# Moving the scan's short matrix products within the steps of a fused scan and feed-forward kernel

## The chip, the core and the metric

The kernel runs on one core of a Trainium2 chip. The metric is the device time of one execution in microseconds (us). A profiled execution also has a span, the time from its first to its last instruction. Engines are named as in the profile: PE multiplies matrices (PEld is its loading of the stationary operand), DVE, ACT and POOL work element by element, SP issues DMA transfers.

## The reference

A state-space scan feeds a feed-forward layer with a cosine gate. There are 4 sequences, 8 heads, 768 positions, 32 channels a head and a state of 16:

```python
for c in range(nc):
    L = np.exp(cum[:, :, :, None] - cum[:, :, None, :]) * causal
    M = np.einsum('bhin,bhjn->bhij', Cc, Bc) * L
    y[:, :, sl] = (np.einsum('bhij,bhjd->bhid', M, xc)
                   + np.einsum('bhin,bhnd->bhid', Cc, state) * np.exp(cum)[:, :, :, None])
    state = decay_full * state + np.sum(Bx, axis=2)
...
h = x @ w_in                 # 3072 x 256 times 256 x 2048
g = h * np.cos(h)
out = g @ w_out              # 3072 x 2048 times 2048 x 256
```

The x of the second part is the y of the first, with heads side by side. All is in float32.

## The kernel before, in words

The 768 positions are cut into 6 chunks of 128, each of two units of 64 positions. For each chunk c the feed-forward layer takes 16 steps f, numbered n = 16 c + f. While the steps of chunk c run, the scan of chunk e = c + 1 is worked out between their instructions. The order on every engine is written out by hand: an engine takes its instructions in the order in which the program issues them.

**One step (period7, from n = 33 on).** The products of a step are done in a form with 7 multiplications in place of 8 (Strassen's), for the first matrix (hp) and for the second (o). Step n begins hp of step n (begin7, L775: three products), then issues the first two products of o of step n - 3 (first_, L846), the last two of hp of step n - 1 (rest7[n - 1][2]), then o's next (then), the middle two of hp of step n (rest7[n][0]), and o's rest (last_). On the other engines the step finishes n - 1: ACT rounds hp to whole turns (wind_k, L682), DVE subtracts (wind_w, L688), ACT takes the sine (gate, L697), DVE multiplies (gated, L702: gT), POOL forms differences (L727, L729, L730: gd). For its own hp, ACT copies partial sums (L779, L780) and DVE adds them (L783, L785). On DVE the order in a step is wind_w(n - 1), L783 and L785 of n, gated(n - 1).

**Banks.** hp of steps 11, 12, 13 and 14 lie in two banks by turns, so begin7 of step 13 waits until gT of step 11 is done, and step 14 until that of step 12. Step 5 waits for gT of step 3. hp of steps 9, 10 and 15 lie in two pairs of banks that y and g use too: y's first pair is that of step 9, its second that of step 10.

**The scan's visits.** Products of the scan are short (64 columns and fewer) and come in groups of 32, which the profile shows as 64 passes. Step 5 holds inner2 (L614: g = B C of both units). Step 13 holds open2 (L628: y from the state and rT, the decayed C; then sums, L478: the new states, not for the last chunk), which stands ahead of begin7. take_ahead (L490) has ACT copy those states. finish2 (L640: y from the masked weights m) has two halves, one before last_ and one behind it, each followed by take_y (L649, ACT copies y to yT), the first also by differ_y (L757, POOL). A visit in the text is what steps 5 and 12 to 14 of one chunk hold: visit A is that of c = 2, B of c = 3, C of c = 4; C has no sums.

**Work beside it.** scan_work lists by step what else the scan does: turn_blocks (L585, DVE transposes), mask_c (L592, ACT), reaches (L575, DVE scan), reach_c (L597, DVE: rT), add_state (L501 and L503, DVE: state), weights (L466, DVE: m), half_decay (L376, DVE: half a scan of decays; its last quarter also issues load_arow, a POOL memset at L162 and two transfers on SP at L164, and weigh0 on POOL, L382). load_blocks (L146, L149) brings B and C in pieces, one a step. The sums of a finished o are added on POOL (L891), one a step, and stored by SP (L894).

Of the kernel before, what the change touches and what calls it, by code (L numbers as in the profile page):

```python
# [25 lines left out]
def kernel(  # L26
# [13 lines left out]
    V, ACT, G, PE = nc.vector, nc.scalar, nc.gpsimd, nc.tensor  # L40
# [3 lines left out]
    P = 128  # L44
    NC = S // P
    DM, DF = moe_w_in.shape
    KT = DM // P
    NF = DF // P
# [573 lines left out]
    def open2(c):  # L622

        ys[c] = y = [pair("y") for _ in range(2)]
        for k, p, s, q in ((k, p, s, q) for k in range(2) for p in range(2) for s in range(2)
                           for q in range(4)):
            r, o_, i = group(q, s), W * (q % 2), (2 * k + p) * W
            PE.matmul(y[s][o_:o_ + W, q // 2, i:i + W], lhsT=after[2 * c + k - 1][r, s, p],  # L628
                      rhs=rTs[c, s][r, p, k * W:(k + 1) * W], start=(k == p == 0), stop=False,
                      tile_position=(r.start, o_), skip_group_check=True)  # L630
        for k in range(2 if c < NC - 1 else 0):
            sums(2 * c + 1 + k, [y[s][:, 0, (2 + k) * P:(3 + k) * P] for s in range(2)], group)

    def finish2(c, ks=(0, 1)):

# [453 lines left out]
        gate(n)  # L1089
        gated(n)  # L1090

    def period7(n, extra=(), begin=(), early=(), end=((), ())):

        for do in begin:
            do()
        begin7(n, bank_of(n))
        while finished:
            finished.pop()()
        first_, then, last_ = seven(n - LAG)
        first_()  # L1100
        if n - 1 in sevens:
            rest7[n - 1][2]()
            wind_k(n - 1)
        then()
        rest7[n][0]()
        for do in early:
            do()
        if n - 1 in sevens:
            wind_w(n - 1)
        rest7[n][1]()  # L1110
        if n - 1 in sevens or n - 1 in late:
            gate(n - 1)
            gated(n - 1)
        for do in end[0]:
            do()
        last_()
        for do in end[1]:
            do()
        for do in extra:
            do()  # L1120

# [52 lines left out]
    for n in range(AHEAD, 2 * NF):  # L1174
        c, f = divmod(n, NF)
        if n < NC * NF:

            if c == 1 and 6 <= f <= 9:
                load(c + 2, f - 6)
            if n in (NF - 4, NF - 3):  # L1180
                load_arow(n - NF + 8)
            if n == NF - 2:
                for k in (4, 5):
                    for s in range(2):
                        load_x(k, s)
            if n in (NF - 1, NF):
                load_along(2, (2 * (n == NF), 2 * (n == NF) + 1))
            for e, i in chunks_at(n, "along"):
                load_along(e + 1, (2 * i, 2 * i + 1))
            first(n)  # L1190
            closing = n == 2 * NF - 1
            if closing:
                finish2(c + 1)
            wind_k(n)
            wind_w(n)
            if closing:
                take_y(c + 1, 0)
            for e, s in chunks_at(n - 1, "turn"):
                turn2(e, s)
            for k in units_at(n, 2):  # L1200
                turn_unit(k)
            if n + 1 in piece:
                rests_of.append(grade(*piece[n + 1], later=True))
            gate(n)
            while len(rests_of) > (n == AHEAD):
                rest = rests_of.pop(0)
                if rest:
                    rest()
            joins = n in piece and piece[n] in held
# [12 lines left out]
            if not joins and behind:  # L1222
                behind.pop(0)()
            gated(n)
            if closing:
                take_y(c + 1, 1)
                take_ahead(c + 1)
                for i in range(4):
                    differ_y(2, i, G, slice(0, 1))
            if n == NF + 7:  # L1230
                weigh0(5)
            if add_s and (n == NF - 5 or units_at(n - 1, 4)):
                exchange = add_s()
                add_s = None
            if n == NF + 9:
                exchange()
            for do in behind:
                do()
            if f not in ((10, 11, 12) if c == 1 else (10, 11)):
                for do in unsummed:  # L1240
                    do()
                unsummed.clear()
            for k, ((_, last_), *_) in unit_at.items():
                if last_ == n:
                    weigh0(k)
        for i, js in differ_at.get(n, ()):
            differ_w(i, js)
        for at in in_at.get(n, ()):
            differ_in(*at)
        if n == AHEAD + 1:  # L1250
            second(n - LAG)
        if n > AHEAD and n != LATER:
            second(n - (LAG if n > LATER else LAG - 1))
        for e, _ in chunks_at(n, "inner"):
            inner2(e)
        for k in units_at(n, 3):
            for t in range(2):
                inner(k, t)
            if k == 3:
                at = [gs[k, s][:, 0, 2 * P:] for s in range(2)]  # L1260
                sums(4, at, group)
                take_sums((4,), at)
            weights(k, 0)
        for k in units_at(n, 4):
            take_s, add_s = finish0(k)
            take_s()
        for k in units_at(n, 1):
            reach_unit(k)
        if n == 2 * NF - 3:
            open2(c + 1)  # L1270
        load_more(n)

    def visit_g(n, e):

        period7(n, begin=[lambda: inner2(e)],
                early=[lambda: weights(2 * e, 0), lambda: weights(2 * e + 1, 0),
                       lambda: weights(2 * e, 1)])

    def visit_y(n, e):

        halves = [lambda i=i: half_decay(2 * e + 3, i // 2, i % 2)
                  for i in range(4 if e < NC - 1 else 0)]

        def taken(k):
            finish2(e, (k,))
            take_y(e, k)
            if k == 0:
                for i in range(4):
                    differ_y(e, i, G, slice(0, 1))

        period7(n, halves[3:], begin=[lambda: open2(e), lambda: take_ahead(e)],
                early=halves[:3], end=[[lambda k=k: taken(k)] for k in range(2)])

    def half_decay(k, p, i):

# [7 lines left out]
    def scan_work(c, f):  # L1303
# [9 lines left out]
                7: [lambda: add_state(2 * e, (1,))],  # L1313
                11: [lambda: turn_blocks(e + 1, 0, (1,))],
                12: [lambda: turn_blocks(e + 1, 0, (0,))]}
        if c == 2:
            work[0] = [lambda: add_state(5), lambda: turn_blocks(e, 0)]
            work[1] = [lambda: turn_blocks(e, 1, (1,)), lambda: mask_c(e, 0, 0),
                       lambda: mask_c(e, 0, 1)]
            work[2] = [lambda: turn_blocks(e, 1, (0,)), lambda: mask_c(e, 1, 0),  # L1320
                       lambda: mask_c(e, 1, 1)]
            work[3] = [lambda: reaches(e, 0)]
            work[4] = [lambda: reaches(e, 1)]
            work[6] = [lambda: weights(2 * e + 1, 1), lambda: reach_c(e, 0)]
            work[7] = [lambda: add_state(2 * e, (0,))]
            work[11] = [lambda: add_state(2 * e, (1,)), *work[11]]
            work[12] = [lambda: reach_c(e, 1), *work[12]]
        for i in range(4 if e < NC - 1 else 0):
            work.setdefault(7 + i, []).append(lambda i=i: half_decay(k, i // 2, i % 2))
        if e == NC - 1:  # L1330
# [4 lines left out]
    for n in range(2 * NF, NC * NF + LAG):  # L1335
# [8 lines left out]
        extra = scan_work(c, f) if live else ()  # L1344
        if n >= NC * NF:
            second(n - LAG)
        elif live and f == 5:
            visit_g(n, e)
        elif live and f == 13:
            visit_y(n, e)  # L1350
        elif n in sevens:
            period7(n, extra)
        else:
            first(n, rest7[n - 1][2] if n - 1 in sevens else None, to_=bank_of(n))
            if n - 1 in sevens:
# [48 lines left out]
```

## Time and profile before

| | |
|---|---|
| median of 3 runs | 368.54 us (368.35 to 368.97) |
| the profiled execution | 368.55 us |
| its span | 366.5 us, so 2.05 us lie around it |
| mean granted clock of PE | 0.995 |
| PE busy | 354.1 us |
| PEld, DVE, ACT, POOL busy | 330.1, 273.2, 213.9, 252.5 us |

The profile of the execution gives its instructions with start and duration, and in brackets the idle time of the engine just before one and what ended it. "issue" there means that the engine waited for nothing that the profile shows. One product of 128 columns appears as two passes, each a weight load and a matmul. A windows line gives, for a stretch of the span, its length, the busy time of PE, PEld, DVE, ACT and POOL with the number of instructions, PE's granted clock, the share of the DMA engines and GB/s. Times in the text are microseconds from the start of the span; times "from the start of step 12" count from 171.71 in visit A, 233.26 in B and 290.52 in C.

### The profile page before, as it was taken

What the parts mean: (1) busy time and instruction counts of PE and PEld (TensorE: products, weight loads), DVE (VectorE), ACT (ScalarE), POOL (GpSimd) and SP (SyncE); (2) the same over time, 40 slices, a digit from 0 to 9 for tenths busy, and PEclk for the clock granted to TensorE, in tenths of its full rate; (3) what the DMA queues carried; (4) which work ended last, traced back from release to release, by engine and by line L of the source; (5) the groups of instructions that cost most, each with busy time, mean ns of one, the idle gap of its engine ahead of it and who ended that gap; (6) DMA issues with size and microseconds to landing.
All of it is one profiled execution on the core that took longest, in us unless ns stands there. A gap on an engine that the chain in (4) does not pass through costs nothing.

```text
span 366.5 us, 10731 instructions
## 1 busy us (share of the span) xinstructions
PE 354.1 (97%) x4268; PEld 330.1 (90%) x4268; DVE 273.2 (75%) x479; ACT 213.9 (58%) x446; POOL 252.5 (69%) x410
## 2 busy tenths in 40 slices
PE   8999999999999999999599999989999999999995
PEld 5788888898989899999599999989999989999995
DVE  7799998578687947898558889868887646666663
ACT  4588766454455267467356756656746746666751
POOL 6567667879869987957555765765776565685671
PEclk9999999999999999999989999999999999999999
DMA  7996957673765147023307103101001001001011
GB/s 142 289 341 147 209 134 90 121 115 76 137 91 92 41 99 96 10 65 75 75 13 104 25 0 71 27 4 38 0 2 31 2 2 31 3 0 30 2 29 29
DMA packets 97328, 26.46 MB, mean 72 GB/s; under 512 B 87328, under 2 KB 93184, under 8 KB 97280
## 3 DMA queue, kind: packets, MB, share of 16 engines
q1 hardware_dynamic: 96032, 25.41, 34.7%
q8 instruction: 33, 0.54, 0.7%
q10 hardware_dynamic: 1248, 0.39, 0.5%
q14 instruction: 15, 0.12, 0.1%
HBM read 22.38 MB, written 3.34 MB: 70 GB/s over the span
## 4 chain that ended last, share of the span: by engine, by line
PE 77%; DVE 6%; POOL 5%; SPq 4%; ACT 4%; issue 3%; DMA 1%; DVEq 0%; POOLq 0%; ACTq 0%
PE o L846 26%; PE hp L775 19%; PE hp L675 17%; PE o L805 7%; DVE gT L702 2%; PE y L640 2%; POOL gd L727 2%; SPq L188 2%; ACT w L697 2%; DVE w L688 2%; SPq L149 1%; ACT k L682 1%; PE y L478 1%; POOL gd L729 1%; POOL gd L730 1%
## 5 line engine op out<-in xcount | busy, mean ns | idle before, releaser
L688 DVE SCALAR_TENSOR_TENSOR w<-hp,k 128x512 f32<-128x512 f32 x96 | 66.0, 688 | 63.4 <-ACT k L682 62.8
L727 POOL TENSOR_TENSOR gd<-gT 128x256 f32<-128x256 f32 x79 | 63.7, 806 | 70.6 <-DVE gT L702 60.2
L697 ACT ACTIVATE w<-w,quarter 128x512 f32<-128x512 f32 x96 | 69.3, 722 | 67.6 <-DVE w L688 67.5
L682 ACT ACTIVATE k<-hp 128x512 int32<-128x512 f32 x96 | 57.4, 598 | 39.2 <-PE hp L675 25.1
L702 DVE TENSOR_TENSOR gT<-hp,w 128x512 f32<-128x512 f32 x96 | 66.0, 687 | 17.7 <-ACT w L697 13.5
L846 PE MATMUL o<-words,gd 128*128 128x128 f32 x474 | 76.6, 277 | 0.0
L675 PE MATMUL hp<-yT,w_in 128*128 128x256 f32 x280 | 66.8, 383 | 0.3 <-DVE gT L702 0.3
L846 PEld LDWEIGHTS o<-words,gd 128*128 128x128 f32 x474 | 64.3, 192 | 0.3 <-issue 0.2
L775 PE MATMUL hp<-m,wid 128*128 128x128 f32 x366 | 61.1, 276 | 0.2 <-ACT hp L780 0.2
L675 PEld LDWEIGHTS hp<-yT,w_in 128*128 128x128 f32 x280 | 51.4, 190 | 7.9 <-POOL mag L250 0.7
L846 PE MATMUL o<-w_out,gT 128*128 128x128 f32 x316 | 49.7, 276 | 2.0 <-issue 2.0
L775 PEld LDWEIGHTS hp<-m,wid 128*128 128x128 f32 x366 | 50.6, 192 | 0.4 <-ACT hp L780 0.3
L775 PE MATMUL hp<-yT,w_in 128*128 128x128 f32 x244 | 48.1, 279 | 2.9 <-DVE gT L702 1.7
L846 PEld LDWEIGHTS o<-w_out,gT 128*128 128x128 f32 x316 | 43.3, 192 | 3.0 <-issue 2.2
L729 POOL TENSOR_TENSOR gd<-gT,gd 128x128 f32<-128x128 f32 x79 | 39.2, 496 | 6.2
L730 POOL TENSOR_TENSOR gd<-gT,gd 128x128 f32<-128x128 f32 x79 | 38.0, 481 | 6.2
L775 PEld LDWEIGHTS hp<-yT,w_in 128*128 128x128 f32 x244 | 37.2, 192 | 4.0 <-issue 1.8
L779 ACT COPY m<-hp 128x256 f32<-128x256 f32 x61 | 22.5, 368 | 15.9 <-PE hp L775 15.5
L846 PE MATMUL o<-w_out,gd 128*128 128x128 f32 x158 | 30.8, 277 | 0.0
L846 PE MATMUL o<-words,gT 128*128 128x128 f32 x158 | 30.8, 277 | 0.0
L805 PE MATMUL o<-w_out,gT 128*128 128x256 f32 x128 | 29.9, 379 | 0.0
L376 DVE TENSOR_TENSOR_SCAN lam<-arow,unit 128x256 f32<-128x256 f32 (+1 forms) x28 | 29.3, 1058 | 0.0
(126 smaller groups left out, 557.2 us busy)
## 6 DMA issues: line engine op xcount, KB each, us to landing
words<-in_moe_w_in_dram SPq DMA_DIRECT2D x8, 512.0 KB
words<-in_moe_w_out_dram SPq DMA_DIRECT2D x8, 512.0 KB
xr<-in_x_dram SPq DMA_DIRECT2D x24, 128.0 KB
arow<-a_cut SPq DMA_DIRECT2D x10, 256.0 KB
arow<-a_cut SPq DMA_DIRECT2D x10, 252.0 KB
out_dram<-sum SPq DMA_DIRECT2D x18, 128.0 KB
bc<-in_B_dram SPq DMA_DIRECT2D x24, 64.0 KB
along<-a_all SPq DMA_DIRECT2D x8, 65.0 KB
```

Source lines behind the costliest of these rows:

```text
L376: V.tensor_tensor_scan(out=lams[k][:, p, hs].rearrange(flat), data0=rows_.rearrange(flat), data1=unit0[:, hs].rearrange(flat), initial=0.0 ...
L675: PE.matmul(to_[:, e], lhsT=w_in[:, k, fs], rhs=y[:, k], start=(k == 0), stop=(k == KT - 1), skip_group_check=True)
L682: ACT.activation(k, hp[n], AF.Copy, bias=0.25, scale=INV_2PI)
L688: V.scalar_tensor_tensor(out=w, in0=hp[n], scalar=INV_2PI, in1=k, op0=ALU.mult, op1=ALU.subtract)
L697: ACT.activation(cos, cos, AF.Sin, bias=quarter, scale=TWO_PI)
L702: V.tensor_tensor(out=gT[n], in0=hp.pop(n), in1=cos, op=ALU.mult)
L727: G.tensor_tensor(out=d[:, 0:2], in0=g[:, 1:2].to_broadcast([P, 2, P]), in1=g[:, 3::-3], op=ALU.subtract)
L729: G.tensor_tensor(out=d[:, 2], in0=g[:, 0], in1=d[:, 0], op=ALU.subtract)
L730: G.tensor_tensor(out=d[:, 3], in0=g[:, 2], in1=d[:, 2], op=ALU.subtract)
L775: PE.matmul(at[:, i], lhsT=w[q], rhs=y_[q], start=(q == 1), stop=True, skip_group_check=True)
L805: PE.matmul(o[c, u][:, t], lhsT=g[:, 2 * e + t], rhs=w_out[:, 2 * j + e], start=(j == e == t == 0), stop=(j == NJ - 1 and e == 1), skip_gr ...
L846: PE.matmul(at[q], lhsT=a_[q], rhs=w[q], start=(j == 0 and q in starts), stop=(j == NJ - 1), skip_group_check=True)
```

## The change

- period7 loses its end hooks and gets mid (behind rest7[n - 1][2] and wind_k) and o_first: with it the first two products of o stand ahead of begin7 instead of behind it.
- Step 5: o_first; inner2 stays where it was.
- Step 12: open2 without the sums (L628) runs at mid.
- Step 13: o_first. The sums (L478, now sums2) and take_ahead come ahead of it; the first half of finish2 (L640), its take_y and differ_y run at mid; two of the four half_decay stay early, the third follows the step.
- Step 14: the second half of finish2 and its take_y come first, then the first products of o (o_first); the fourth half_decay follows the step.
- c = 2 alone: reach_c(e, 1) moves from step 12 to step 8, the second half of add_state(2 e) from step 11 to step 9.
- The number of products, copies, scans and transfers is the same. open2 of chunk 2 (n = 29) is followed by its sums as before.

```diff
-        for k in range(2 if c < NC - 1 else 0):
-            sums(2 * c + 1 + k, [y[s][:, 0, (2 + k) * P:(3 + k) * P] for s in range(2)], group)
+    def sums2(c):
+        for k in range(2 if c < NC - 1 else 0):
+            sums(2 * c + 1 + k, [ys[c][s][:, 0, (2 + k) * P:(3 + k) * P] for s in range(2)], group)
...
-    def period7(n, extra=(), begin=(), early=(), end=((), ())):
+    def period7(n, extra=(), begin=(), mid=(), early=(), o_first=False):
+        first_, then, last_ = seven(n - LAG)
         for do in begin:
             do()
+        if o_first:
+            first_()
         begin7(n, bank_of(n))
         while finished:
             finished.pop()()
-        first_, then, last_ = seven(n - LAG)
-        first_()
+        if not o_first:
+            first_()
         if n - 1 in sevens:
             rest7[n - 1][2]()
             wind_k(n - 1)
+        for do in mid:
+            do()
         then()
         rest7[n][0]()
...
-        for do in end[0]:
-            do()
         last_()
-        for do in end[1]:
-            do()
...
+    def visits(n, e):
+        f = n % NF
+        if f == 5:
+            return dict(o_first=True, begin=[lambda: inner2(e)],
+                        early=[lambda: weights(2 * e, 0), lambda: weights(2 * e + 1, 0),
+                               lambda: weights(2 * e, 1)])
+        if f == 12:
+            return dict(mid=[lambda: open2(e)])
+        if f == 13:
+            return dict(o_first=True, begin=[lambda: sums2(e), lambda: take_ahead(e)],
+                        mid=[lambda: finish2(e, (0,)), lambda: take_y(e, 0)] + [
+                            lambda i=i: differ_y(e, i, G, slice(0, 1)) for i in range(4)],
+                        early=[lambda i=i: half_decay(2 * e + 3, 0, i)
+                               for i in range(2 if e < NC - 1 else 0)])
+        return {}
...
+        for i in range(2 if e < NC - 1 else 0):
+            work.setdefault(13 + i, []).append(lambda i=i: half_decay(2 * e + 3, 1, i))
...
-            work[11] = [lambda: add_state(2 * e, (1,)), *work[11]]
-            work[12] = [lambda: reach_c(e, 1), *work[12]]
+            work[8] = [lambda: reach_c(e, 1)]
+            work[9] = [lambda: add_state(2 * e, (1,))]
...
         elif n in sevens:
-            period7(n, extra)
+            at = visits(n, e) if live else {}
+            if f == 14 and c >= 2 and c < NC - 1:
+                at = dict(o_first=True, begin=[lambda: finish2(e, (1,)), lambda: take_y(e, 1)])
+            period7(n, extra, **at)
```

More of the change, by code (lines that the diff above doesn't have):

```diff
@@ L1270 @@
             open2(c + 1)
+            sums2(c + 1)
         load_more(n)
[L1273 to L1292, printed above, removed]
+    def visits(n, e):
[13 more added lines that the diff above has]
+        return {}
     def half_decay(k, p, i):
@@ L1346 @@
             second(n - LAG)
[L1347 to L1350, printed above, removed]
         elif n in sevens:
-            period7(n, extra)
+            at = visits(n, e) if live else {}
+            if f == 14 and c >= 2 and c < NC - 1:
+                at = dict(o_first=True, begin=[lambda: finish2(e, (1,)), lambda: take_y(e, 1)])
+            period7(n, extra, **at)
         else:
```

## The prediction

> **What bounds the kernel now.** I read the page first, then the waits, then each visit in the timeline of PE.
>
> ```profile
> span 366.5 us, 10731 instructions
> ...
> PE 354.1 (97%) x4268; PEld 330.1 (90%) x4268; DVE 273.2 (75%) x479; ACT 213.9 (58%) x446; POOL 252.5 (69%) x410
> ...
> q8 instruction: 33, 0.54, 0.7%
> ```
>
> PE is full, so the question is where its few idle microseconds lie. Busy time by stretches (length, PE, PEld, DVE, ACT, POOL, clock, DMA) shows it: steps 12 to 14 of visits A, B, C, then step 5 of A, a step without a visit, and a stretch of A.
>
> ```profile
> 171.70:190.50 18.80, 15.07 (x343) 13.79 (x342) 10.79 (x22) 8.16 (x21) 12.12 (x22) 0.91 0.29 62
> 233.26:247.74 14.48, 13.29 (x343) 12.63 (x341) 10.41 (x20) 8.14 (x21) 10.40 (x18) 1.00 0.04 10
> 290.50:303.75 13.25, 12.60 (x279) 11.88 (x278) 6.25 (x14) 7.00 (x17) 9.06 (x18) 1.00 0.02 4
> 147.77:152.63 4.86, 4.51 (x95) 4.20 (x93) 4.64 (x9) 1.94 (x4) 4.62 (x9) 1.00 0.02 4
> 152.63:155.75 3.12, 3.12 (x30) 3.12 (x29) 2.03 (x5) 1.95 (x5) 2.96 (x6) 1.00 0.00 0
> 183.20:186.60 3.40, 3.40 (x93) 2.79 (x99) 2.62 (x5) 1.45 (x4) 0.90 (x1) 0.50 0.00 0
> ```
>
> A and B do the same work, yet A takes 4.3 us more. PE's timeline names the idle times (in brackets): A's two, B's, C's, and A's step 5 (B and C have 0.36 and 0.37 there).
>
> ```profile
> 176.97 0.84 PE L628 MATMUL y<-rT,state 32*64 32x64 f32 x56 [1.69 <-DVE rT L597]
> ...
> 181.72 0.49 PE L846 MATMUL o<-w_out,gT 128*128 128x128 f32 x2 [2.04 <-issue]
> ```
> ```profile
> 237.32 0.86 PE L478 MATMUL y<-xr,sc 64*32 64x64 f32 x64
> 239.37 0.38 PE L775 MATMUL hp<-yT,w_in 128*128 128x128 f32 x2 [1.19 <-issue]
> ```
> ```profile
> 295.30 0.46 PE L775 MATMUL hp<-yT,w_in 128*128 128x128 f32 x2 [0.65 <-DVE gT L702]
> ```
> ```profile
> 149.43 0.46 PE L775 MATMUL hp<-yT,w_in 128*128 128x128 f32 x2 [0.35 <-DVE gT L702]
> ```
>
> The two "issue" waits are code. Queue 8 brings 33 packets of 16 KB for PE's 8641 entries (4268 loads, 4268 matmuls, 105 waits). Counted in the trace, the waits end at entries 4289 and 5826: 1537, or 6 x 256 + 1, apart, so code comes in blocks of 256. The packets ran 179.19 to 180.34 and 236.95 to 237.83; PE went on 1.37 and 1.54 us after their ends. Where PE crosses other block edges among short products, the next packet starts 0.60 to 1.00 us later (209.96, 298.27, 244.01, 186.89). In A it took 2.2 us; packets of 252 bytes (arow) held the DMA from 176 to 179.2. From one edge to a usable next block is thus 2.9 (B) to 4.7 us (A); L628 and L478 together, 1.6 us, are just one block of 256.
>
> **Prices.** A pass of a long product takes 0.1115 (28 in 3.12). Passes of L628 take 0.84 in all, of L478 0.79 (177.73 to 178.52), of the halves of L640 0.79 and 0.95. Each island of short products costs 0.2 more: 0.1 at its entry (236.38 to 236.48), and its first two long passes behind it take 0.33 instead of 0.22.
>
> **Step 5, three times.** Nothing is added. L614 ends 1.2 after the step's start, hp's bank is free at 1.66. Four first passes of o put between them (0.45) bring the arrival to 0.1 + 1.14 + 0.55 = 1.79: the wait goes, and the step takes 3.12 + 0.1 + 1.14 + 0.11 = 4.48 instead of 4.86. **-0.38 each, -1.1 in all**; the margin is 0.13, and without it the 0.38 shrink by what gT is later.
>
> **Steps 12 to 14, PE alone.** A and B: 3 x 3.13 + 0.84 + 0.79 + 0.79 + 0.95 + 4 islands x 0.2 = 13.56. There is one island more than before (L628 and L478 were one). C, without L478: 12.57. Against 18.78 (171.71 to 190.49), 14.48 and 13.23 that is -5.22, -0.92, -0.66, if nothing waits. Of A's 5.2, 1.69 is rT, 2.04 code, and 1.7 the half clock of 3.4 us. What can wait, counted from the start of step 12:
>
> *rT and state (A).* DVE does L597 (0.41) in step 8 and L503 (0.41) in step 9 instead of 12 and 11. There its only idle times from 159.9 to 167.5 are the 0.19 ahead of each L702, then come 0.29 and 0.45; so it is up to 0.5 late until step 11 and then level. Behind it waits gd of step 8 on POOL, over at 169.16, then 169.6; PE takes it at 170.2. Cost 0; if that 0.6 is gone, up to 0.4.
>
> *The bank of the second y.* open2 now runs at 1.67 and needs step 10's gT, whose L702 ends at 234.93 - 233.26 = 1.67, plus 0.1 for the signal. PE reaches that bank at 1.77. I take 0.05 for A, 0 for B and C; ends 0 and 0.3.
>
> *hp in step 13.* open2 lengthens step 12, so L783 and L785 of step 12 start at about 3.75 (3.0 before) and L702 of step 11, behind them on DVE, ends at 5.2 instead of 4.63; the bank is free at 5.35. In A and B PE arrives at 4.17 + 0.99 (L478) + 0.55 (o) = 5.7: no wait. In C there is no L478: it arrives at 4.62 and waits 0.73 where it waited 0.65. So C gains 0.66 - 0.73 = **-0.07, that is nothing**. If L702 were as early as now (4.78 free), the wait would be 0.16 and C would gain 0.5. I take 0.73, since DVE's order puts the sums first.
>
> *hp in step 14.* L702 of step 12 ends near 10.4 (wind_w behind PE's 6.84, then sin behind take_y, then the sums at 9.0); PE arrives at 9.42 + 0.9 + 0.65 = 10.97. No wait; o's first passes are the cover, without them 0.1.
>
> *take_ahead* (ACT, 1.14) ends at 6.4 before the first L640 at 6.9. *differ_y* (POOL, 4 x 0.47) now stands ahead of step 12's gd (1.7), which is ready at 12.3 and used at 15.1.
>
> *Half scans, arow, SP.* Two scans stay in step 13 and two move behind steps 13 and 14; DVE idles there (0.85 and 2.06 in B). With A's last go POOL's memset (0.12) and L382 (0.64), past one gd. Its two arow transfers now queue on SP behind the store of the sums (190.61 now, about 184.7 then) and a pair of C blocks, instead of running at 174.81. The pair behind them lands near 192.6; DVE transposes it at 201.33 - 4.9 = 196.4. Cost 0.
>
> *Code.* In A the edge now falls 46 entries into L628. To the next edge PE has 0.54 + 0.1 + 14 x 0.1115 + 0.1 + 0.79 + 0.1 + 0.9 = 4.1 us. It needs 2.9 to 4.7; the other arow pair (issued 169.92, packets 171 to 175) lies under this fetch. Ends 0 and 2.04 as now; nearest is a packet that starts at 175.2 when these end: 177.8 against 177.75, and I take 0.3. In B it is 0.64 + 0.1 + 1.56 + 0.1 + 0.79 = 3.2 against 2.9 (B itself) or 3.6: I take 0.15, ends 0 and 0.7. In C blocks last over 6 us: 0.
>
> *Clock.* A idled 1.69 + 2.04 within 6.8 us, and the half clock began at 183.2; B's 1.19 brought none. With 0.35 left in A I take it as gone; ends 0 and 1.7.
> [...] The trace shows a half-clock stretch of 3.41 us after gaps of 1.69 and 2.04, and I follow it.
> [...]
>
> **Sum.** -1.1 (step 5) - 5.22 + 0.05 + 0.3 (A) - 0.92 + 0.15 (B) - 0.07 (C) = -6.8, off the profiled execution's own 368.55 (span 366.5 and 2.05 around it): **361.8**. The median, 368.54, is the same.
>
> **Rivals.**
> 1. *Code runs dry again in A.* For it: the arow packets at 171 to 175, and A's margin is nil. Against: 4.1 us of cover instead of 1.6. 1.0 to 2.0 more: about 363.2; chance 0.17. With the half clock too 1.7 more, 365 (0.06).
> 2. *Cleaner:* no code wait, and C's L702 early: 361.8 - 0.45 - 0.5 = 360.9; chance 0.14.
> 3. *Nothing comes of it:* code waits move with the products, rT was only the last of several causes, and only step 5 gains: 367.5 to 369; chance 0.03.
> 4. *Slower.* open2 stands in front of step 12's own products. If step 10's gT comes late to its bank, PE stands, all of step 12 with it, and the clock falls: 2.04 + 1.7 a visit as in A now, 11.2 for three, 361.8 + 11.2 = 373. It decides from 2.3 us of wait a visit, or 0.6 with the clock. For it: the arrival is level with the release. Against: both come from PE's own pace, within 0.1 in three visits. Chance 0.04.
>
> The forecast itself has 0.55 (361.2 to 362.6), 0.01 is left over. 0.2% is about what a measurement of this kernel can tell from no change: faster 0.93, same 0.03, slower 0.04. The range, 360.8 to 364.0, takes in the forecast, the cleaner case and rival 1 without the clock.
>
> **What would show it.** Right: 4.5 us for the steps with L614; no PE wait on L597; clock 1.00 throughout; A and B 13.6 to 14.0 each; C 13.2 with a wait of about 0.7 on gT. Wrong: an "issue" wait over 0.5 in A or B, a wait in front of L628's second bank, or a half-clock stretch.

## The result

The changed kernel takes **364.48 us** (median of 4 runs, 364.01 to 366.13) against 368.69 before; the ratio is 0.9894, 95% interval 0.986 to 0.9929. It is faster, as forecast, but by 4.2 us and not by 6.8: the time lies 0.5 above the upper end of the range. The profiled execution of the changed kernel took 364.01 us, with 2.41 us around its span. Its line numbers from L675 on are 3 higher than in the kernel before: L678, L691, L705, L730, L778, L788, L849 were L675, L688, L702, L727, L775, L785, L846. The page of the profile and its queue 8:

```profile
span 361.6 us, 10733 instructions
...
PE 353.6 (98%) x4268; PEld 329.6 (91%) x4268; DVE 273.4 (76%) x479; ACT 213.0 (59%) x446; POOL 251.9 (70%) x410
...
q8 instruction: 33, 0.54, 0.6%
```

The busy times changed by less than 1 us; PE idles 8.0 us in place of 12.4, and A's stretch of half clock, which counts as busy, is gone too. The windows view of the changed kernel shows steps 12 to 14 of A, B and C (length, PE, PEld, DVE, ACT, POOL, clock, DMA):

```profile
172.62:186.24 13.62, 13.62 (x342) 12.76 (x341) 9.63 (x19) 8.03 (x20) 11.37 (x20) 1.00 0.17 38
229.01:242.72 13.71, 13.53 (x342) 12.78 (x341) 9.67 (x19) 8.09 (x20) 11.08 (x20) 1.00 0.04 10
285.49:298.73 13.24, 12.82 (x278) 12.01 (x277) 6.20 (x14) 6.94 (x16) 9.55 (x18) 1.00 0.01 2
```

A is as short as B. But PE has a wait that the prediction does not know, on DVE's sums (L788): two of its four times are in steps 10 and 11 of A, two in step 6 of B and C. PE's waits (us in total, times, longest), of the steps in question:

```profile
PE hp L778 <- DVE hp L788: 1.0, 4, 0.3
...
PE hp L778 <- DVE gT L705: 0.4, 1, 0.4
...
PE o L849 <- issue: 0.2, 1, 0.2
```

To find where the time went, I took the end of each step as the start of its last pass of o, and compared step by step. From the end of step n = 36 on, the lengths repeat to some hundredths between executions, save where code or transfers come late (us; A, B, C as above; "5+6 B" is the same in C to 0.02; "36 to the end" runs to the last pass of o in the last step, and every length is of the one profiled execution):

| kernel | 5 A | 10+11 A | 12–14 A | 12–14 B | 12–14 C | 5+6 B | 36 to the end | median | ratio to before, 95% |
|---|---|---|---|---|---|---|---|---|---|
| before | 4.85 | 6.25 | 18.78 | 14.48 | 13.23 | 8.26 | 213.03 | 368.69 | |
| changed | 4.57 | 7.21 | 13.63 | 13.71 | 13.25 | 8.26 | 207.77 | 364.48 | 0.9894, 0.986–0.9929 |
| again | 4.57 | 7.21 | 13.62 | 13.72 | 13.25 | 8.26 | 207.82 | 364.61 | 0.9859, 0.9807–0.991 |
| swap | 4.57 | 7.12 | 13.62 | 13.65 | 13.26 | 8.25 | 207.68 | 364.03 | 0.9881, 0.9852–0.991 |
| spread | 4.57 | 6.25 | 13.88 | 13.66 | 13.25 | 8.26 | 207.05 | 363.54 | 0.9857, 0.9833–0.9881 |
| third | 4.57 | 7.21 | 13.62 | 13.72 | 13.25 | 7.70 | 206.64 | 362.73 | 0.9846, 0.9821–0.9871 |
| before_rt | 4.86 | 7.20 | 13.67 | 14.28 | 13.23 | 8.27 | 208.67 | 366.04 | 0.9887, 0.9837–0.9937 |
| rt_alone | 4.85 | 6.25 | 14.08 | 14.53 | 13.23 | 8.26 | 208.35 | 364.70 | 0.9844, 0.9805–0.9883 |
| arow_late | 4.86 | 6.25 | 16.85 | 14.28 | 13.23 | 8.26 | 210.87 | 366.67 | 0.9892, 0.9852–0.9932 |
| before_shift | 4.85 | 6.25 | 16.76 | 13.52 | 13.23 | 8.27 | 210.03 | 373.33 | 1.0125, 1.01–1.0149 |
| join | 4.57 | 7.21 | 13.93 | 13.72 | 12.74 | 8.27 | 207.61 | 363.76 | 0.9833, 0.9789–0.9878 |
| best | 4.57 | 6.25 | 13.88 | 13.89 | 13.25 | 7.70 | 206.15 | 362.47 | 0.9792, 0.9748–0.9836 |
| best2 | 4.58 | 6.25 | 13.88 | 13.92 | 12.74 | 7.70 | 205.66 | 363.04 | 0.98, 0.9757–0.9842 |
| best3 | 4.57 | 6.25 | 13.78 | 13.81 | 12.74 | 7.70 | 205.46 | 362.08 | 0.981, 0.9763–0.9857 |

Each ratio is to runs of before on the same chip; their medians went from 368.69 to 371.23, so ratios taken on different chips differ by more than the steps do. The steps tell the kernels apart.

**The account of the 5.26 us from step 36 on.** Visits A, B, C lost 5.15, 0.77 and gained 0.02. Step 5 of A lost 0.28. Steps 10 and 11 of A took **0.96 more**; no term of the sum has them. In B and C step 5 lost 0.29 (4.87 to 4.57) and step 6 took 0.29 more (3.40 to 3.69): nothing was left. -5.15 - 0.77 + 0.02 - 0.28 + 0.96 = -5.22; the other 0.04 is rounding and small differences in other steps. Ahead of step 33, where both kernels are the same, this execution was 0.35 slower, and 0.36 more lay around its span: -5.26 + 0.35 + 0.36 = -4.55, from 368.55 to 364.0. The median of the four executions lies 0.47 above this one.

**Where the 0.96 is.** PE's timeline of the changed kernel, steps 10 and 11 of A:

```profile
167.01 0.49 PE L778 MATMUL hp<-yT,wid 128*128 128x128 f32 x2 [0.21 <-DVE hp L788]
...
170.61 0.49 PE L778 MATMUL hp<-yT,wid 128*128 128x128 f32 x2 [0.20 <-DVE hp L788]
```

This is rest7[n - 1][2], the last two products of hp of the step before: they add into hp behind DVE's sums. The brackets show only part of the loss: PE could have gone on 0.45 after 166.19 and starts 0.37 later than that, at 167.01, and its first two passes then take 0.33 instead of 0.22. That is 0.48 a step, twice. What DVE did ahead of them, and POOL's gd beside it, then DVE in the same step of the kernel before:

```profile
163.54 0.69 DVE L705 TENSOR_TENSOR gT<-hp,w 128x512 f32<-128x512 f32 x1 [0.19 <-ACT w L700]
164.15 0.41 DVE L597 TENSOR_TENSOR rT<-turned,reach 128x256 f32<-128x256 f32 x1
164.48 1.22 DVE L376 TENSOR_TENSOR_SCAN lam<-arow,unit 128x256 f32<-128x256 f32 x1
```
```profile
164.38 0.77 POOL L730 TENSOR_TENSOR gd<-gT 128x256 f32<-128x256 f32 x1 [1.49 <-DVE gT L705]
```
```profile
164.09 0.68 DVE L376 TENSOR_TENSOR_SCAN lam<-arow,unit 128x256 f32<-128x256 f32 x1
```

rT (L597) costs DVE not 0.41 but 0.87: 0.33 from its start to that of the next, and 0.54 more because it pushes the half scan (L376, 0.68 right behind gT) under POOL's gd, where it takes 1.22. Behind it wind_w (165.62) and the sums (166.21, 166.66) are late, and PE stands.

The kernel before has this very wait once, in step 9 of A, which takes 3.45 there. It follows steps 6 and 7, in each of which DVE has two instructions of the scan behind gT:

```profile
163.34 0.30 PEld L775 LDWEIGHTS hp<-yT,wid 128*128 128x128 f32 x2 [0.25 <-DVE hp L785]
```

So DVE had no room left where the change put rT and the state.

### The profile page after: what moved, and what is told of

It reads as the page before. It is cut to its first block, busy times and chain, and to the rows that moved or that the text cites. A ratio compares the mean times of both kernels' runs of the same rounds, so it can differ in the third digit from the quotient of the medians.

```text
span 361.6 us, 10733 instructions
## 1 busy us (share of the span) xinstructions
PE 353.6 (98%) x4268; PEld 329.6 (91%) x4268; DVE 273.4 (76%) x479; ACT 213.0 (59%) x446; POOL 251.9 (70%) x410
## 4 chain that ended last, share of the span: by engine, by line
PE 81%; DVE 10%; ACT 4%; issue 1%; DMA 1%; POOL 1%; SPq 0%; DVEq 0%; POOLq 0%; ACTq 0%
PE o L849 28%; PE hp L778 21%; PE hp L678 17%; PE o L808 7%; DVE w L691 2%; DVE gT L705 2%; ACT w L700 2%; PE y L643 2%; DVE m L466 1%; DMA bc<-in_B_dram 1%; DVE rT L597 1%; DVE lam L376 1%; ACT k L685 1%; PE y L628 1%; PE y L478 1%
## 5 line engine op out<-in xcount | busy, mean ns | idle before, releaser
L730 POOL TENSOR_TENSOR gd<-gT 128x256 f32<-128x256 f32 x79 | 63.5, 804 | 65.3 <-DVE gT L705 53.1
L691 DVE SCALAR_TENSOR_TENSOR w<-hp,k 128x512 f32<-128x512 f32 x96 | 65.9, 687 | 55.8 <-ACT k L685 55.2
L705 DVE TENSOR_TENSOR gT<-hp,w 128x512 f32<-128x512 f32 x96 | 65.9, 686 | 16.0 <-ACT w L700 10.4
L849 PE MATMUL o<-words,gd 128*128 128x128 f32 x474 | 76.6, 277 | 0.0
L678 PE MATMUL hp<-yT,w_in 128*128 128x256 f32 x280 | 66.8, 383 | 0.3 <-DVE gT L705 0.3
L849 PEld LDWEIGHTS o<-words,gd 128*128 128x128 f32 x474 | 64.1, 192 | 0.5
L778 PE MATMUL hp<-m,wid 128*128 128x128 f32 x366 | 61.7, 277 | 0.2 <-ACT hp L783 0.2
L678 PEld LDWEIGHTS hp<-yT,w_in 128*128 128x128 f32 x280 | 51.4, 190 | 8.0 <-POOL mag L250 0.7
L778 PEld LDWEIGHTS hp<-m,wid 128*128 128x128 f32 x366 | 50.6, 192 | 0.7 <-ACT hp L783 0.3
L849 PE MATMUL o<-w_out,gT 128*128 128x128 f32 x316 | 50.1, 277 | 0.2 <-issue 0.2
L778 PE MATMUL hp<-yT,w_in 128*128 128x128 f32 x244 | 47.2, 275 | 0.4 <-DVE gT L705 0.4
L849 PEld LDWEIGHTS o<-w_out,gT 128*128 128x128 f32 x316 | 43.3, 192 | 1.9 <-issue 0.5
L778 PEld LDWEIGHTS hp<-yT,w_in 128*128 128x128 f32 x244 | 37.0, 192 | 0.6 <-issue 0.6
L849 PE MATMUL o<-words,gT 128*128 128x128 f32 x158 | 30.5, 275 | 0.0
L849 PE MATMUL o<-w_out,gd 128*128 128x128 f32 x158 | 30.5, 275 | 0.0
L376 DVE TENSOR_TENSOR_SCAN lam<-arow,unit 128x256 f32<-128x256 f32 (+1 forms) x28 | 30.4, 1090 | 0.0
```

The lines of the kernel that those rows point to most:

```text
L376: V.tensor_tensor_scan(out=lams[k][:, p, hs].rearrange(flat), data0=rows_.rearrange(flat), data1=unit0[:, hs].rearrange(flat), initial=0.0 ...
L678: PE.matmul(to_[:, e], lhsT=w_in[:, k, fs], rhs=y[:, k], start=(k == 0), stop=(k == KT - 1), skip_group_check=True)
L691: V.scalar_tensor_tensor(out=w, in0=hp[n], scalar=INV_2PI, in1=k, op0=ALU.mult, op1=ALU.subtract)
L705: V.tensor_tensor(out=gT[n], in0=hp.pop(n), in1=cos, op=ALU.mult)
L730: G.tensor_tensor(out=d[:, 0:2], in0=g[:, 1:2].to_broadcast([P, 2, P]), in1=g[:, 3::-3], op=ALU.subtract)
L778: PE.matmul(at[:, i], lhsT=w[q], rhs=y_[q], start=(q == 1), stop=True, skip_group_check=True)
```

## The experiments

Four theories were tested: that rT and the state cost the 0.96 (again, swap, spread); that the third of the weights takes step 5's gain back (third); what made A's loss in the kernel before, the wait on rT, code, arow transfers or the clock (before_shift, before_rt, rt_alone, arow_late); and what open2's new place is worth (join, best2, best3). best puts the two repairs together.

**again**: the changed kernel, unaltered.

> The changed kernel once more, unaltered. Theory: what the forecast missed lies in four steps that repeat to a few hundredths (A's steps 10 and 11 at 3.60 each where 3.13 was reckoned, step 6 of B and C at 3.69 where 3.40 stood before), and 207.8 us from the end of step 36 to the end; what differs between executions is the part ahead of step 33, by up to about 1 us, and so the median lies between 363.5 and 365. Rival: the miss was one disturbed execution; then steps 10 and 11 show 3.13 here and the median is near 362.

Each group of steps in the table repeats within 0.01 to 0.02. The median is 364.61 (363.72 to 366.62). Ahead of step 36 this profile is 1.14 slower than the first one of the same kernel. So the steps are the kernel's own and the rival fell; what varies is the start.

**swap**: in A's steps 8 and 9 the half scan goes ahead of rT and the state.

```diff
+        if c == 2:
+            for i in (8, 9):
+                work[i].reverse()
```

> Only the order of two scans on DVE changes in visit A: in steps 8 and 9 the half scan (L376) runs before rT and the state's addition instead of behind them. Theory (collision): in the changed kernel the half scans behind rT and the addition start while POOL's gd already runs and take 1.22 instead of 0.68, and this 0.54 a step, not the 0.41 of rT and of the addition alone, is what makes DVE too late for PE's third part of hp in steps 10 and 11. Then the half scans of steps 8 and 9 return to about 0.7, PE's steps 10 and 11 lose 0.0 to 0.5 instead of 0.95, and the time falls by 0.4 to 0.9 against the changed kernel. Rival (load): DVE is late because 0.82 more work stands in steps 8 and 9 whatever the order; then steps 10 and 11 still lose 0.8 to 1.0 and the time is the same as the changed kernel's within 0.2.

The theory (the order) fell and the rival (the load) held: steps 10 and 11 still lose 0.87 of the 0.96. The half scans are back at 0.68, and now the second instruction is the slow one, 0.89 in place of 0.41 (the state in step 9 too). DVE of swap in step 8:

```profile
165.09 0.68 DVE L376 TENSOR_TENSOR_SCAN lam<-arow,unit 128x256 f32<-128x256 f32 x1
165.69 0.89 DVE L597 TENSOR_TENSOR rT<-turned,reach 128x256 f32<-128x256 f32 x1
```

Whichever of the two comes second behind gT meets gd, which gT has just let go, and takes about 0.5 more. The order cures next to nothing; two such instructions in one step are the load.

**spread**: rT in step 10, the state in step 11.

```diff
-            work[8] = [lambda: reach_c(e, 1)]
-            work[9] = [lambda: add_state(2 * e, (1,))]
+            work[10] = [lambda: reach_c(e, 1)]
+            work[11] = [lambda: add_state(2 * e, (1,)), *work[11]]
```

> In visit A rT is made in step 10 and the state added in step 11, instead of steps 8 and 9; all else as in the changed kernel. Theory (DVE too late for PE's third part of hp): steps 10 and 11 of A return to 3.13 (0.95 less), the state is ready about 2.0 after the start of step 12, level with the second half of L628, which waits 0 to 0.2; the time falls by 0.7 to 0.95. Rival (the 0.95 is not DVE's lateness from these two instructions but comes with the run): steps 10 and 11 lose as much as in the changed kernel. Second rival: the loss only moves, L628 waits 0.5 or more for the state and the time is the same.

Steps 10 and 11 lose nothing (6.25). Step 12 takes 0.25 more: 0.15 ahead of hp's last two products, which wait for sums that end at 174.13, and 0.11 in L628, whose second bank waits for gT of step 10 (174.32 to 175.01). The state, which was expected to be late, is level with its products and adds nothing that can be told apart. PE and DVE of spread:

```profile
174.18 0.49 PE L778 MATMUL hp<-yT,wid 128*128 128x128 f32 x2
...
174.82 1.16 PE L628 MATMUL y<-rT,state 32*64 32x64 f32 x64
```
```profile
171.32 0.41 DVE L597 TENSOR_TENSOR rT<-turned,reach 128x256 f32<-128x256 f32 x1
171.65 1.22 DVE L376 TENSOR_TENSOR_SCAN lam<-arow,unit 128x256 f32<-128x256 f32 x1
...
174.92 0.41 DVE L503 TENSOR_TENSOR state<-state,whole 128x256 f32<-128x256 f32 x1
```

The half scan takes 1.22 here too, but behind steps 8 and 9, which have one such instruction each, the delay is only those 0.25. In the changed kernel steps 8 and 9 came straight behind steps 6 and 7, which hold two in both kernels. Net -0.7: that the place of rT and the state costs the 0.96 is shown (and before_rt, below, has the 0.95 with nothing else changed); that it is the row of four such steps is read from the traces.

**third**: the third of the weights (L466) out of the middle of step 5 to behind it.

```diff
-                        early=[lambda: weights(2 * e, 0), lambda: weights(2 * e + 1, 0),
-                               lambda: weights(2 * e, 1)])
+                        early=[lambda: weights(2 * e, 0), lambda: weights(2 * e + 1, 0)])
...
+        work[5] = [lambda: weights(2 * e, 1)]
```

> In step 5 of all visits the third product of weights (L466, 0.6 on DVE) runs behind the step instead of ahead of wind_w; all else as in the changed kernel. Theory: what step 5 gained in B and C (0.29 each) came back as a longer wait in step 6, where PE's third part of hp waits for L788 of step 5, and that is late by the three L466 ahead of it. Then step 6 of B and C falls from 3.69 to 3.13, step 5 stays at 4.57, and the time falls by 0.9 to 1.1. Rival (the wait in step 6 is set by something that the weights don't delay, such as ACT or the copy of partial sums): step 6 stays at 3.5 to 3.7 and the time is the same within 0.2.

As expected: step 6 of B and C falls from 3.69 to 3.13, step 5 keeps its 4.57: -1.13. In the changed kernel three L466 stand ahead of the sums on DVE, and PE waits in step 6; first DVE, then PE of the changed kernel:

```profile
208.18 1.87 DVE L466 TENSOR_TENSOR m<-g,lam 128x512 f32<-128x512 f32 x3
```
```profile
211.37 0.49 PE L778 MATMUL hp<-yT,wid 128*128 128x128 f32 x2 [0.29 <-DVE hp L788]
```

and in third two, with no wait:

```profile
208.92 1.27 DVE L466 TENSOR_TENSOR m<-g,lam 128x512 f32<-128x512 f32 x2
```

**before_shift**: the kernel before, with 16 short products (64 entries) behind the first filling of PE; they write a spare bank, and move the block edges of all code that follows.

```diff
-    fill(bank([P, 2, P], "warm", "o"))
+    spare = bank([P, 2, P], "warm", "o")
+    fill(spare)
+    for _ in range(16):
+        PE.matmul(spare[0:32, 0, 0:64], lhsT=nc.const_aps.tensor(1.0, (P, 32), FP32),
+                  rhs=nc.const_aps.tensor(1.0, (P, 64), FP32),
+                  start=True, stop=True, skip_group_check=True)
```

> The kernel before, with 16 tiny products added right at the start (64 entries of PE's program, into a bank that nothing reads), so that every later block edge of PE's code falls 64 entries earlier in the work; nothing else changes. Theory (code): the two issue waits of A and B, 2.04 and 1.19, were blocks of 256 entries run through faster than the next one came; with the edges moved, L628 and L478 no longer fill one block, both waits vanish, A keeps its wait of 1.7 for rT, and the half clock of 3.4 us in A goes too, as it needed both waits: 368.6 falls to 363.8 to 365.6, the higher end if the clock still falls. Rival (the waits belong to the short products themselves, or to banks, wherever the block edges are): both waits stay and the time is within 0.5 of the kernel before.

Both code waits are gone (B 13.52; A 16.76, where the wait on rT stays), so it is the place of the block edges that makes them, and the rival fell. That blocks have 256 entries comes from counting: the first late entry is 4289 in A and 5825 in B of the kernel before, 1536 = 6 x 256 apart, the new wait at the start of before_shift is at 705, 14 x 256 ahead of 4289, and queue 8's 33 packets for PE's 8641 entries make 262 a packet. But an edge now falls among short products of the first chunk, and the start loses 7.2 us (154.82 against 147.66), 3.49 of them in this wait and 1.7 in the half clock behind it. PE of before_shift, then the window of A's half clock (the start has one at 22.07 to 25.48):

```profile
22.29 0.43 PE L528 MATMUL y<-m,xr 64*32 64x64 f32 x5 [3.49 <-issue]
...
184.12 0.84 PE L628 MATMUL y<-rT,state 32*64 32x64 f32 x56 [1.69 <-DVE rT L597]
```
```profile
185.91:189.32 3.41, 3.41 (x18) 3.41 (x18) 0.80 (x2) 2.01 (x7) 1.32 (x2) 0.50 0.25 47
```

In A the half clock comes after the wait on rT alone, so it did not need the code wait. The time went up, not down as expected.

**before_rt**: the kernel before with rT and the state in steps 8 and 9, nothing else.

```diff
-            work[11] = [lambda: add_state(2 * e, (1,)), *work[11]]
-            work[12] = [lambda: reach_c(e, 1), *work[12]]
+            work[8] = [lambda: reach_c(e, 1)]
+            work[9] = [lambda: add_state(2 * e, (1,))]
```

> The kernel before with only rT and the state of chunk 2 in steps 8 and 9. Theory: the gap of 1.69 on rT goes, steps 10 and 11 of A take 3.60 each (+0.95), and open2 with the sums stays one block of code, so the code wait in A does not go but takes over: PE comes to the edge earlier while the packet is held as before, a wait of 1.3 (if the packet is free) to 3.7 us (if arow holds it as before), with the half clock behind it if it is over 1.7; B keeps its 1.2. Steps 12 to 14 of A 15.5 to 18.8, the time 366 to 369.5. Rival: rT and code are two separate prices; steps 12 to 14 of A lose 1.69 and the half clock as well (15.4), the code wait stays at 2.04, and the time is 366. Second rival, that rT set off the half clock alone: a wait of over 2 on code and no half clock behind it.

Theory and rivals fell alike: A takes **13.67**, no code wait and no half clock, with open2 and the sums still in one block. PE of before_rt, in A and in B:

```profile
176.82 1.08 PE L628 MATMUL y<-rT,state 32*64 32x64 f32 x64
177.82 0.86 PE L478 MATMUL y<-xr,sc 64*32 64x64 f32 x64
178.61 0.49 PE L775 MATMUL hp<-yT,w_in 128*128 128x128 f32 x2
...
235.84 0.49 PE L775 MATMUL hp<-yT,w_in 128*128 128x128 f32 x2 [0.89 <-PE y L478]
```

B's wait of 0.89 is at entry 5825 too: it is the code wait, though the view names L478. The packet of code came at 176.76, with L628, between two pairs of arow transfers (the queue's records end at 176.60 and begin again at 177.41). In the kernel before it came at 179.19. Counted in the trace of before, the pass that waits for rT there is entry 4032, and the block edge (4289 - 256) is at 4033: PE stood one entry ahead of it. So the packet was asked for only when the wait was over, as far as these times tell, and by then the second arow pair was on its way.

**rt_alone**: one line of the kernel before; rT in step 10, the state stays in step 11.

```diff
-            work[12] = [lambda: reach_c(e, 1), *work[12]]
+            work[10] = [lambda: reach_c(e, 1)]
```

> The kernel before with one line moved: rT of chunk 2 in step 10 instead of step 12, the state left in step 11. Theory: the wait of 1.69 on rT was what started A's whole loss, since it let the second pair of arow transfers get ahead of the packet of code and brought the half clock; without it steps 10 and 11 stay at 3.13, steps 12 to 14 of A take 13.7 (before_rt: 13.67), B keeps 14.3 to 14.5, and from the end of step 36 to the end it is 213.03 - 5.1 = 207.9: as much as the whole change (207.8). Rival: with steps 10 and 11 short again the arow transfers come level with the packet, and a code wait of 0.5 to 2 stays in A: 14.2 to 15.7.

A takes 14.08, between the theory's 13.7 and the rival's 14.2. The packet came in time (175.85 to 176.81), but the arow pair behind it (178.70 to 180.85) met the next one, which came at 180.73 to 181.81; the second half of finish2 then waits 0.16 for yT and takes 1.32 in place of 1.01, within reach of that packet:

```profile
182.14 1.32 PE L640 MATMUL y<-m,xr 64*32 64x64 f32 x64 [0.16 <-ACT yT L649]
```

In the trace the longest pause within these products is 0.29, at entry 4545, 256 entries after the edge at 4289: a small code wait. Step 12 takes 0.14 more as well (3.27). Still, one line gives 213.03 - 208.35 = **4.68 of the 5.26 us** of the whole change (against the profiled execution of the kernel before, with its half clock).

**arow_late**: the kernel before with only the last quarter of the half scan of step 13, and its arow pair, behind step 14.

```diff
-        period7(n, halves[3:], begin=[lambda: open2(e), lambda: take_ahead(e)],
+        period7(n, begin=[lambda: open2(e), lambda: take_ahead(e)],
...
+        if e < NC - 1:
+            work.setdefault(14, []).append(lambda: half_decay(2 * e + 3, 1, 1))
```

> The kernel before with only the last quarter of the half scan of step 13, and with it one pair of arow transfers, moved behind step 14 (as the change does); rT, the products and their order as before. Theory: the arow transfers made A's code wait longer than B's; without them the packet starts 0.6 to 1.0 us after the edge at 176.9 instead of 2.2, PE goes on 1.4 to 1.5 behind its end, at 180.1 to 180.4, and A's code wait is 0.4 to 0.8 in place of 2.04. The wait on rT stays at 1.69 and is enough for the half clock (it was in the kernel with shifted code), so A takes 18.77 - 1.2..1.6 = 17.2 to 17.6. Rival 1: the packet is late for the wait on rT itself, 2.04 stays, 18.8. Rival 2: the half clock needs both waits; then 15.5 to 15.9.

A takes 16.85: no code wait shows, and the half clock stays. PE and the windows of arow_late:

```profile
177.62 0.84 PE L628 MATMUL y<-rT,state 32*64 32x64 f32 x56 [1.69 <-DVE rT L597]
```
```profile
177.60:178.65 1.05, 1.03 (x88) 0.98 (x89) 1.05 (x3) 0.00 (x0) 0.97 (x2) 1.00 0.02 8
178.65:182.05 3.40, 3.40 (x71) 3.13 (x49) 1.56 (x2) 1.76 (x6) 2.00 (x3) 0.50 0.02 5
```

The packet ran 178.76 to 179.95, 1.14 after the wait's end, against 2.22 (179.19 after 176.97) with arow in its way. The half clock (from 178.65) lies over the time in which PE could have waited for code; A is shorter than expected by 0.4, and how long that wait would have been at full clock is not shown. Rival 1 (2.04 stays, for rT's sake alone) fell in its number, though the packet still comes only behind the wait on rT; rival 2 (half clock only after two waits) fell.

**join**: the changed kernel with open2 back ahead of the sums.

```diff
-            return dict(mid=[lambda: open2(e)])
+            return {}
...
-            return dict(o_first=True, begin=[lambda: sums2(e), lambda: take_ahead(e)],
+            return dict(o_first=True, begin=[lambda: open2(e), lambda: sums2(e), lambda: take_ahead(e)],
```

> The changed kernel with open2 back in step 13, directly ahead of the sums; the rest as changed. Theory (code comes in blocks of 256 entries): the next edge is then 2.6 us (A) and 1.6 us (B) behind the one before, where 2.9 to 4.7 are needed; so a code wait of 0.3 to 2.1 in A and of about 1.3 in B, less an island of 0.2 each: 363.9 + 0.1..1.9 + 1.1 = 365 to 367. C has no code wait there, saves the island, and gT of step 11 is ready sooner since step 12 is short, so its wait of 0.42 shrinks to 0.2 or less and C gains 0.3 to 0.5. Rival: the code waits went because rT and arow moved, not because the products were spread; then no code wait in either, and 0.2 less in A, B and C, 363.3.

A code wait of 0.5 comes back in A and B, smaller than reckoned in B, and C takes 0.51 less, as reckoned (0.3 to 0.5). The time, 363.76, is near the rival's 363.3 and not in the 365 to 367 expected: most of the two code waits stays away though open2 and the sums are joined. In A before_rt shows why; why B's fell from 1.19 to 0.47 was not tested. PE of join in A, B and C, then C in the changed kernel:

```profile
180.30 0.49 PE L778 MATMUL hp<-m,wid 128*128 128x128 f32 x3 [0.48 <-issue]
...
236.01 0.60 PE L849 MATMUL o<-w_out,gT 128*128 128x128 f32 x4 [0.47 <-issue]
...
291.89 0.46 PE L778 MATMUL hp<-yT,w_in 128*128 128x128 f32 x2
```
```profile
290.88 0.46 PE L778 MATMUL hp<-yT,w_in 128*128 128x128 f32 x2 [0.42 <-DVE gT L705]
```

By steps the split is worth 0.30 in A, nothing in B and -0.51 in C: join has 207.61, the changed kernel 207.77.

**best** is spread and third together; **best2** has open2 back in step 13 in C alone as well; **best3** has it back in all three.

```diff
-            return dict(mid=[lambda: open2(e)])
+            return dict(mid=[lambda: open2(e)] if e < NC - 1 else [])
...
-            return dict(o_first=True, begin=[lambda: sums2(e), lambda: take_ahead(e)],
+            return dict(o_first=True, begin=([lambda: open2(e)] if e == NC - 1 else []) + [lambda: sums2(e), lambda: take_ahead(e)],
```

> The changed kernel with rT of chunk 2 in step 10 and the state in step 11, and with the third of the weights after step 5 in place of inside it. Theory: the two losses have nothing to do with each other, so the gains add up: A's steps 10 and 11 at 3.13 and step 12 at 4.56 (-0.7), step 6 of B and C at 3.13 (-1.1); 205.95 us from the end of step 36 to the end, and 362.2 us, 1.8 below the changed kernel. Rival: in A step 6 has both (weights, rT's first half), DVE is late again there, and part comes back: A's steps 6 to 8 longer by 0.3 to 0.9, 362.6 to 363.1.

> The best so far, and in C, which has no sums, open2 again directly ahead of step 13. Theory: the wait of 0.42 on gT of step 11 in C comes from the long step 12, so step 12 to 14 of C take 12.74 (as in join) and not 13.25, and all else stays: 205.43 us from the end of step 36 to the end, 362.0 us. Rival: an edge of code moves in among C's products and takes it back: an issue wait in C, 13.0 to 13.3.

> The two repairs (rT and state of chunk 2 in steps 10 and 11, third of the weights behind step 5) with open2 back in step 13 in all three visits: the split of open2 from the sums undone everywhere, the first o products still ahead of hp. Theory: the split is worth nothing in sum, for it wins 0.3 in A (a code wait of 0.48 less an island), nothing in B, and loses 0.5 in C; here A 13.9 as with the split (there L628 waited 0.25 for the state, here for code), B 13.7, C 12.74, and 205.5 us from the end of step 36 to the end, level with the version that keeps the split in A and B (205.66). Rival: with steps 10 and 11 short the packet of code in A meets the arow transfers again, the wait grows to 1 to 2 us and the split is what prevents it: A 14.5 to 15.5, 206.2 to 207.2.

The gains add up and the three rivals fell: 206.15, 205.66 and 205.46, each 0.2 above or level with what was reckoned; the 0.2 of best and best2 is a code wait in B of 0.4 in place of 0.18. best3 is the shortest by steps, 7.57 below before and 2.31 below the changed kernel, at a median of 362.08 us (361.41 to 362.84); by medians best, best2 and best3 can't be told apart.

## Why the prediction was wrong, point by point

- **"rT and state (A). Cost 0; if that 0.6 is gone, up to 0.4": failed, it cost 0.96**. The steps missed by 1.54 (-6.8 against -5.26): 0.96 here, 0.82 in step 5, 0.09 in C, less 0.28 in A; the rest is rounding. Two things in it were wrong. I followed only one waiter, POOL's gd, and found it 0.6 of room; the waiter that bit is PE's own third part of hp, behind the sums L785 (now L788), and the reckoning left it out. And I priced rT and the state at 0.41 each, where each adds 0.87 in front of a half scan. The trace of before showed both: in its step 7, L501 (0.41) is followed by a half scan of 1.22, and in its step 9 PE's loads stand 0.25 for L785.
- **"Step 5, -0.38 each, -1.1 in all": right in mechanism, wrong in size, and blind to what is late next.** Each step 5 gained 0.29. In B and C all of it came back in step 6, which already had a wait of 0.27 for the sums behind three L466; moving PE ahead only makes it meet them sooner. The sum lost 0.82 here (-1.1 against -0.28). A, where DVE has other work there, kept its 0.28. Of the 0.09 that each step 5 gained too little, A's trace shows a cause: with o's first passes moved ahead, hp's middle two products come to ACT's copy L783 (151.18 to 151.43) too early, and their weight loads start at 151.48, 0.12 late.
- **Steps 12 to 14, right.** A 13.63 (13.91 said; the two waits allowed for, 0.05 and 0.3, did not come), B 13.71 (13.71), C 13.25 (13.3; the wait there is 0.42 in the profile's count, 0.58 counted from PE's arrival as the sum does, where 0.73 was said). B's remaining code wait is 0.18 (0.15 said).
- **Why A gained, only half right.** I listed 1.69 (rT), 2.04 (code) and 1.7 (clock) as three losses and credited the spreading with the code. before_rt and rt_alone show one root: rT's wait, one entry ahead of a block edge, held back the packet (179.19, 2.22 after that wait's end), and the half clock came behind it (183.20). Spreading the products did not cure A; by join it is worth 0.30 there. The half clock's part of A's 5.15 belongs to the profiled execution of before: not every execution of that kernel has it (last section).
- **C**: the two halves of the reckoning are shown apart. The rest of the change, o ahead of hp above all, wins 0.49 (join, 13.23 to 12.74; finish2 moved too and was not tried apart), open2 in step 12 gives 0.51 back, by the late gT that I had named.
- **Outside the terms.** The profiled execution of before was the quickest of all the profiles up to the end of step 36 (147.66; the others 148.01 to 149.25 but for before_shift and best2). I took its 368.55 as typical, and by its time it was: the four runs of its kernel took 368.35 to 368.97. The forecast had no room for what lies outside the steps: 361.8 + 1.54 (steps) is 363.3, still within the range, and 0.35 ahead of step 33, 0.36 around the span and 0.47 from this execution to the median make 364.5.
- **The signs.** Those named for being right came (4.57 in step 5, no wait on L597, clock 1.00, A and B at 13.6 and 13.7, C at 13.2, if with a shorter wait), and none of those for being wrong did. The list left out steps 10 and 11 of A and step 6 of B and C, where the loss was.

Of DVE beside gd the rows show times alone: gd starts at 164.38; L597, begun ahead of it at 164.15, takes 0.41, and the half scan, begun behind it at 164.48, takes 1.22, or 0.54 more than its 0.68. In swap gd starts at 165.32; the half scan, begun at 165.09, takes 0.68, and L597, begun at 165.69, takes 0.89, or 0.48 more than its 0.41. Why the one begun behind gd takes longer, no run shows.

## What to carry to other kernels

When work moves to another step, list every reader of what its engine does next, PE's accumulating products among them, and price the moved instruction together with its neighbour, as it stands in a step that already holds such a pair. Look in the kernel before for the wait that the move would lengthen: here it stood in step 9 already. A gain on one engine counts only up to the next thing that is already nearly late. And try the smallest part of a change alone: here one moved line gave 4.68 of 5.26 us.

## What the runs showed of the hardware

**The clock.** A stretch of half clock of 3.40 to 3.41 us followed a single wait of 1.69 in A (before_shift and arow_late, beginning 1.8 and 1.0 after it). The profiled execution of best2 had a longer one near the start without it: DVE's transpose waited for a transfer, PE stood 2.20, and the clock stayed at 1.00. DVE, PE and a window of best2:

```profile
107.69 0.63 DVE L585 STREAM_TRANSPOSE turned<-blocks 128x256 f32<-128x256 f32 x1 [2.99 <-DMA blocks<-in_C_dram]
```
```profile
109.29 2.00 PE L678 MATMUL hp<-yT,w_in 128*128 128x256 f32 x8 [2.20 <-DVE gT L705]
```
```profile
108.00:112.00 4.00, 2.71 (x61) 2.23 (x68) 3.98 (x6) 2.23 (x4) 2.85 (x4) 1.00 0.62 110
```

So the length of the wait alone does not decide. Nor does the program: one such stretch in 366.5 us makes a mean granted clock of 0.995, and of the 44 executions of the kernel before that were timed beside the experiments 9 have 0.998 or more, 17 have 0.993 to 0.995, and 18 have 0.984 to 0.991, as low as two to three and a half such stretches would make it (an estimate from the mean alone). arow_late has 0.995 in its profiled execution and 1.00 in its other five; all six of before_shift have 0.989 or 0.990. No execution of any kernel in which rT was moved is below 0.998. But for the one at the start of before_shift, then, a whole stretch of half clock came only in kernels that have the wait on rT, as far as these means tell, and there not each time; what decides stays open.

**The start.** The lines of best2 also show one thing that makes the time before step 36 differ from execution to execution: a block of C that lands late (DVE stood 2.99 for it). What makes the smaller differences, up to 1.6 us, is not known.

**Code.** In before_shift one block edge among short products of the first chunk cost 3.49 us, more than the two waits that went with the shift (2.04 and 1.19): where the edges fall is set by the code ahead, of which 64 entries more were enough here.
